# A half unit's start: TensorE's own count in place of a pass through ScalarE, and sums of h by either engine

## Chip, cores and metric

The kernel runs on one core of a Trainium2 chip. The metric is device time in microseconds (us) for one execution. A core has five engines with a queue each, which work side by side and wait for each other through semaphores: TensorE (PE in the profile, with its weight loads as PEld), VectorE (DVE), ScalarE (ACT), GpSimd (POOL) and SyncE (SP, which issues the DMAs).

## What is computed

One transformer layer with attention and an MLP in parallel, on 2048 tokens of width 512; 32 heads of 16, hidden width 1792:

```python
xn = _layernorm(x, axis=-1)
return x + _A_ref(xn, A_wqkv, A_wo) + _B_ref(xn, B_w1, B_b1, B_w2, B_b2)
# _A_ref: scores = q @ k.T * Dh**-0.5; p = softmax(scores); o = p @ v; o @ wo
# _B_ref: h = gelu(xn @ w1 + b1); h @ w2 + b2
```

## The kernel before

Attention is cut into 512 *units*: a group of four heads, a block of 512 queries, a block of 128 keys. For each unit the scores are formed twice. S (`s_half`, four a unit, one per head) has queries on the partitions; DVE takes the row maximum from PSUM (L226). Twenty units later (LEAD) T (`e_half`) forms the transposed scores with the maximum folded in, ACT takes the exponential into a tile pe (L273), and V (`v_half`) multiplies it with the values and adds up over 16 units in one PSUM bank. V is in fp32 and runs as two passes in the trace.

Beside that runs *dense* work, D: groups of products that add up in a bank of their own. In order of time they are 24 groups of the q and k projections, the MLP in four blocks of tokens (14 groups for h, then four for the output y), and the output projection. `Group.pace` says how many D products a half unit takes: four, or three (FAST, MEAN, SLOW). All products use 64 rows of the PE array and 32 columns at a time, so that each shows as four tiles, and two row halves work side by side.

`unit` (L551) writes the order by hand. A unit has two halves; I call each a *block*. A block issues S, T, S, T, then V on one row half of the array and D on the other. In the next block the halves change over. So V and D of a block add into the same banks as those of the block before, from other rows, and must not start before those are finished. For this, an empty instruction is put on DVE or ACT at the end of each block (L579), whichever has the smaller count of work given (`backlog`, from which HALF = 1300 ns is taken per block). It waits for the newest product on PE (L580), and the next block's first product of V or D waits for it (`fence`, L166 to L169). It stands in the engine's queue behind that engine's earlier work.

S and T rotate over three PSUM banks each; D has one, V one. When a D group ends, its bank goes to T's list (`Group.end`), with ACT or DVE still to read it. For h this is `hidden` (L952): DVE scales hp and adds the bias into hh, then ACT and GpSimd do the gelu in later slots.

Of the kernel before, what the change touches and what calls it, by code (L numbers as in the profile page):

```python
# [8 lines left out]
F32 = mybir.dt.float32  # L9
# [8 lines left out]
P = 128  # L18
# [29 lines left out]
def layer_kernel(ctx: ExitStack, tc: tile.TileContext, x, wqkv, wo, w1, b1, w2, b2, out):  # L48
# [43 lines left out]
    nc.gpsimd.memset(vv[:, :, 0:H * VW].rearrange("p t (h e) -> p t h e", e=VW)[:, :, :, DH], 1.0)  # L92
    nc.gpsimd.memset(vv[:, :, H * VW:], 0.0)
    wo_s = const.tile([P, 2, NC, D], F16, name="wo_s")
    wo_l = const.tile([64, 2, D], F16, name="wo_l")
    sexp = const.tile([P, 4], F32, name="sexp")

    mnegs = [const.tile([P, 32], F32, name=f"mneg{i}") for i in range(2)]
# [55 lines left out]

    PAIRS = ((0, 0), (0, 1), (1, 0))

    AFTER = mybir.DependencyInfo(mybir.DependencyClass.Sync, mybir.DependencyReason.DATA)
    fence, newest = [None], [None]

    backlog = {"act": 0, "dve": 0}  # L160

    def given(engine, ns):
        backlog[engine] += ns

    def product(*args, **kw):
        newest[0] = nc.tensor.matmul(*args, **kw)  # L166
        if fence[0] is not None:
            tc.add_manual_dep(newest[0].ins, fence[0].ins.name, AFTER, reason="other rows")
            fence[0] = None  # L169

    def tiled(dst, lhs, rhs, start, stop):

        for j in range(0, P, 32):
            product(dst[j:j + 32], lhs[:, j:j + 32], rhs, start=start, stop=stop)


    mt_of, ptiles, pv_of = {}, {}, {}
# [36 lines left out]
    def s_half(u, n):  # L214

        t, i = divmod(u, 16)
        g, qb = divmod(t, NQB)
        qt, kb = divmod(i, 4) if t else (i % 4, i // 4)
        if t not in mt_of:
            mt_of[t] = work.tile([P, 4, 4, 4], F32, name="mt", bufs=2)  # L220
        ks, qs = kst[g % 2], qst[g % 2]
        p, a = divmod(n, 2)
        r = slice(64 * a, 64 * a + 62)
        s = banks("S")
        tiled(s, qs[p][qb][r, qt * P:(qt + 1) * P], ks[p][kb][r, :], True, True)
        nc.vector.reduce_max(mt_of[t][:, n, qt, kb:kb + 1], s, axis=AX.X)  # L226
        given("dve", 600)

# [33 lines left out]
    def e_half(u, n):  # L262

        p, a = divmod(n, 2)
        t, kt = divmod(u, 16)
        g, qb = divmod(t, NQB)
        st = banks("T")
        r = slice(64 * a, 64 * a + 64)
        k0 = (kt % 4) * P
        tiled(st, kst[g % 2][p][kt // 4][r, k0:k0 + P], qst[g % 2][p][qb][r, :], True, True)  # L270
        pe = work.tile([P, QB], F32, name="pe", bufs=10)
        ptiles[u, n] = pe
        nc.scalar.activation(pe, st, AF.Exp, scale=sexp[:, g // 2:g // 2 + 1])  # L273
        given("act", 580)

    def v_half(u, a):

        t, kt = divmod(u, 16)
        g, qb = divmod(t, NQB)
        if kt == 0 and a == 0:  # L280
            pv_of[t] = hold("V", "S")
        pv = pv_of[t][0]
        r = slice(64 * a, 64 * a + 64)
        for h in (2, 3, 0, 1):
            c = (4 * g + h) * VW
            product(pv[32 * h:32 * h + 32, :], vv[r, kt, c:c + 32], ptiles[u, h][r],
                    start=(kt == 0 and a == 0), stop=(kt == 15 and a == 1))

    def v_end(u):
# [90 lines left out]
    class Group:  # L380
# [15 lines left out]
        def product(self, side):  # L396

            if self.bank is None:
                self.bank, self.key = self.alloc()
            lhs, rhs = self.prods[side % 2][self.at[side % 2]]()  # L400
            start = self.first and self.at == [0, 0]
            if side == 2:
                self.at = [min(self.at[0] + 1, n) for n in self.n]
                nc.tensor.matmul(self.bank, lhs, rhs, start=start, stop=self.last and self.over())  # L404
                return
            r = slice(64 * side, 64 * side + 64)
            self.at[side] += 1
            tiled(self.bank, lhs[r], rhs[r], start, self.last and self.over())

        def over(self):  # L410
            return self.at == self.n
# [40 lines left out]
    def project(m, w, sb, wh, bank, early=False):  # L452

        prods = [lambda c=c, i=i, j=j: (wh[:, w, i, c, :], xt[:, j, c, sb * QB:(sb + 1) * QB])
                 for c in range(NC) for i, j in PAIRS]

        dst = qk_d[w, m * P:(m + 1) * P, :, sb * QB:(sb + 1) * QB]

        def finish(pj):
            def put():  # L460
                nc.sync.dma_start(dst[:, w:w + 2, :], stg)
                nc.sync.dma_start(dst[:, 2 - 2 * w, :], stg[:, 0])

            stg = work.tile([P, 2, QB], F16, name="stg", bufs=2)
            given("act", 600)
            if early or (w == 1 and not m):
                nc.scalar.activation(stg[:, 0], pj, AF.Copy)
                nc.vector.tensor_tensor(stg[:, 1], pj, stg[:, 0], op=ALU.subtract)
            else:
                pf = ph.tile([P, QB], F32, name="pf", bufs=2)  # L470
                nc.scalar.activation(pf, pj, AF.Copy)
                if not m:
                    nc.scalar.activation(stg[:, 0], pj, AF.Copy)
                    nc.gpsimd.tensor_tensor(stg[:, 1], pf, stg[:, 0], op=ALU.subtract)
                else:
                    hi = lambda: nc.gpsimd.tensor_scalar(stg[:, 0], pf, 1.0, 0.0, op0=ALU.mult, op1=ALU.add)
                    lo = lambda: nc.gpsimd.tensor_tensor(stg[:, 1], pf, stg[:, 0], op=ALU.subtract)
                    later(1, lambda: pooled((620, hi), (1160, lo), (0, lambda: later(1, put, True))), True)
                    return

            put()

        return Group(prods, bank, finish)
# [62 lines left out]
                    cur[0].product(side)  # L546
        ended()

    passed_by = [None]

    def unit(gen):  # L551


        u = pos[0]
        e = u - LEAD
        if u == LEAD and cur[0] is not None:
            burst(gen, cur[0].left())
        pos[0] += 1
        for a in range(2):
            for b in range(2 * a, 2 * a + 2):  # L560
                if u < NU:
                    s_half(u, b)
                if 0 <= e < NU:
                    e_half(e, b ^ 1)
            if e >= 0:
                fence[0] = passed_by[0]

                w, r = (e - 2, 1) if a == 0 else (e - 1, 0)
                live = 0 <= w < NU
                new = r == 0 and w % 16 == 0  # L570
                if live and not new:
                    v_half(w, r)
                dense(gen, 1 - r)
                if live and new:
                    v_half(w, r)

                for k in backlog:
                    backlog[k] = max(0, backlog[k] - HALF)
                passed_by[0] = (nc.vector if backlog["dve"] < backlog["act"] else nc.scalar).nop()  # L579
                tc.add_manual_dep(passed_by[0].ins, newest[0].ins.name, AFTER, reason="block")  # L580
                if live and r == 1:
                    v_end(w)
                ended()
        if u < NU:
            s_end(u)
        if u < LEAD:
            burst(gen, LFILL[u - 16])
        tick()
# [9 lines left out]
    with ExitStack() as st1:  # L598
# [240 lines left out]
        def prepare():  # L839
# [20 lines left out]
            for n in range(16):  # L860
                v = fetch(16 + n)
                while not ended[0]:
                    yield
                ended[0] = False

                def then(wh=None, n=n):
                    ended[0] = True
                    if n < 7:
                        for a in range(2):
                            for l in range(2):  # L870
                                nc.sync.dma_start(w1_d[2 * n + a][:, l], wh[:, l, :, a * P:(a + 1) * P])
                    elif n < 14:
                        nc.sync.dma_start(w2_d[:, :, 2 * n - 14:2 * n - 12, :], wh)
                    elif n == 15:
                        nc.sync.dma_start(wo_l, wo_s[64:128, :, NC - 1, :])

                if n >= 14:
                    i = 2 * (n - 14)
                    split_steps(wo_s[:, 0, i:i + 2, :], wo_s[:, 1, i:i + 2, :], v, inv[:, 9:10], then)
                    continue  # L880
                wh = ph.tile([P, 2, 4, W] if n < 7 else [P, 2, 2, D], F16, name="wsp", bufs=2)
                k = n if n < 7 else 8
                split_steps(wh[:, 0], wh[:, 1], v, inv[:, k:k + 1], lambda wh=wh, then=then: then(wh))
# [12 lines left out]
    def mlp():  # L896
# [43 lines left out]
        for b in range(NQB):  # L940
            xb = xbs[b]
            g = m2.tile([P, 2, NF, QB], F16, name="g", bufs=1)
            for f in range(NF):
# [8 lines left out]
                def hidden(hp, g=g, b=b, f=f):  # L952
                    hh = m2.tile([P, QB], F32, name="hh", bufs=3)
                    scale, bias = fac1[0][:, f // 2:f // 2 + 1], b1_s[:, f:f + 1]
                    nc.vector.tensor_scalar(hh, hp, scale, bias, op0=ALU.mult, op1=ALU.add)  # L955
                    given("dve", 700)
                    later(1, lambda: gelu(hh, g, b, f), True)

                yield Group([lambda c=c, i=i, j=j, wc=wc, xb=xb: (wc[:, i, c, :], xb[:, j, c, :])
# [74 lines left out]
        flush()  # L1034
    with ExitStack() as st3:
        p3 = pool(st3, "ph3")

        blocks = {}

# [64 lines left out]
```

## Time and profile before

| | |
|---|---|
| median of 3 runs | 1587.66 us (1586.63 to 1590.76) |
| the profiled execution | 1592.59 us, its span 1590.8 us |
| row maximum, L226 on DVE | 2048 of them, 1293.2 us busy |
| exponential, L273 on ACT | 2048 of them, 1270.1 us busy |
| V on PE, L166 | 8192 rows (4 tiles, two passes), 1083.3 us busy |
| hh, L955 on DVE | 56 of them, 45.4 us busy |

A group's row gives busy time, mean duration in ns and, behind the bar, the idle time of its engine just before it and what ended that. A timeline row gives start, duration, engine, line, operation, out<-in, shape and count, and in brackets idle time and its releaser. "who waited" rows give total and count. Nearly all matmuls have line L166, since a helper issues them; the tile's name tells them apart (pS, pT, pV, pD).

### The profile page before, as it was taken

Reading aid. Unit: us, or ns where it says so; the run is one execution under the profiler, and the core shown is the slowest. Engines: PE = TensorE matmul, PEld = TensorE weight load, DVE = VectorE, ACT = ScalarE, POOL = GpSimd, SP = SyncE. Lnnn points to the kernel's source line nnn. Section 1 sums busy time; section 2 is a strip of 40 time slices with the busy share of each in tenths; the row PEclk is TensorE's granted clock in tenths of the full one; section 3 lists DMA queues with packets and bytes.
Section 4 is the critical chain, followed back from the end, with each engine's and each line's share of the span. In section 5 each row is a group of like instructions: output and inputs, shape, how many; then the busy total and the mean of one; then the engine's idle time right before and its main releaser. Section 6 shows DMA issues by size and latency. Waiting matters only on the chain.

```text
span 1590.8 us, 86996 instructions
## 1 busy us (share of the span) xinstructions
PE 1535.3 (97%) x38915; PEld 807.7 (51%) x38915; DVE 1424.0 (90%) x2388; ACT 1378.9 (87%) x2254; POOL 668.7 (42%) x742
## 2 busy tenths in 40 slices
PE   8997998999999999999999999999999999999998
PEld 4433554545555555555455555555555555554443
DVE  7896987989999999999899999999999999999901
ACT  4315997989999999999899999999999999999893
POOL 3113586727773111677411157681116775211000
PEclk9999999999999999999999999999999999999999
DMA  6466375361112111121111111221112110103222
GB/s 204 136 210 210 108 190 184 124 197 53 44 54 64 35 34 31 55 60 46 46 38 48 33 53 41 61 67 33 33 46 59 41 34 15 39 23 97 91 95 82
DMA packets 120256, 123.78 MB, mean 78 GB/s; under 512 B 38988, under 2 KB 90572, under 8 KB 119880
## 3 DMA queue, kind: packets, MB, share of 16 engines
q1 hardware_dynamic: 119880, 118.21, 24.6%
q8 instruction: 304, 4.98, 1.3%
q14 instruction: 72, 0.59, 0.1%
HBM read 80.61 MB, written 37.34 MB: 74 GB/s over the span
## 4 chain that ended last, share of the span: by engine, by line
PE 80%; DVE 10%; DMA 4%; POOL 2%; issue 2%; SPq 1%; ACT 1%; DVEq 0%; ACTq 0%; POOLq 0%
PE pV L166 25%; PE pD L166 18%; PE pT L166 17%; PE pS L166 16%; DVE mt L226 6%; DVE hh L955 2%; PE pD L404 1%; DMA wch<-in_B_w_dram 1%; PE pT L404 1%; DVE amx L614 1%; DMA dn<-den_d 1%; PE pT L497 1%; ACT pe L273 0%; DMA m_d<-mhl 0%; DMA xb<-xn_d 0%
## 5 line engine op out<-in xcount | busy, mean ns | idle before, releaser
L226 DVE TENSOR_REDUCE mt<-pS 128x1 f32<-128x512 f32 x2048 | 1293.2, 683 | 59.4 <-PE pS L166 34.3
L273 ACT ACTIVATE pe<-pT,sexp 128x512 f32<-128x512 f32 x2048 | 1270.1, 686 | 77.5 <-PE pT L166 27.9
L166 PE MATMUL pV<-pe,vv 64*32 64x512 f32 x8192 | 1083.3, 599 | 1.9 <-ACTq L579 0.8
L166 PE MATMUL pT<-qst,kst 64*32 64x512 f16 x8192 | 708.1, 379 | 11.3 <-DMA qst<-m_d 8.2
L166 PE MATMUL pS<-kst,qst 62*32 62x512 f16 x8192 | 640.9, 379 | 28.0 <-DVE mt L226 24.1
L166 PEld LDWEIGHTS <-qst 62*32 62x32 f16 x8192 | 271.5, 92 | 253.2 <-issue 123.0
L166 PEld LDWEIGHTS <-kst 64*32 64x32 f16 x8192 | 290.9, 91 | 209.4 <-issue 80.2
L166 PE MATMUL pD<-w_s,g 64*32 64x512 f16 x5376 | 365.4, 379 | 0.0
L166 PE MATMUL pD<-xb,wc 64*32 64x512 f16 x5376 | 360.9, 378 | 0.2 <-issue 0.2
L166 PEld LDWEIGHTS pV<-pe,vv 64*32 64x32 f32 x8192 | 177.0, 105 | 122.4 <-ACTq L579 25.4
L166 PEld LDWEIGHTS <-wc 64*32 64x32 f16 x5376 | 117.4, 92 | 46.0 <-issue 2.3
L166 PEld LDWEIGHTS <-g 64*32 64x32 f16 x5376 | 106.9, 92 | 44.2 <-issue 0.7
L166 PE MATMUL pD<-xt,wqk_h 64*32 64x512 f16 x1920 | 127.4, 381 | 0.7 <-issue 0.7
L973 POOL TENSOR_TENSOR xa<-xa,yt 128x512 f32<-128x512 f32 x16 | 20.4, 1276 | 242.9 <-ACT yt L971 242.9
L935 POOL TENSOR_TENSOR t<-hh 128x512 f32<-128x512 f32 x56 | 58.2, 1039 | 119.3 <-DVE hh L955 117.8
L324 POOL TENSOR_TENSOR osb<-osb,rb 128x512 f32<-128x512 f32 x31 | 39.8, 1284 | 157.0 <-DMA rb<-den_d 115.1
L250 POOL TENSOR_SCALAR mhl<-msb 64x64 f16<-64x64 f32 x32 | 7.6, 236 | 178.4 <-DVE msb L247 178.4
L937 POOL TENSOR_TENSOR t<-t,hh 128x512 f32<-128x512 f32 x56 | 71.7, 1280 | 4.7
L930 POOL TENSOR_TENSOR t<-t,hh 128x512 f32<-128x512 f32 x56 | 71.5, 1277 | 4.7
L932 POOL TENSOR_TENSOR g<-t,g 128x512 f16<-128x512 f32 x56 | 65.1, 1163 | 4.4
L166 PE MATMUL pD<-wo_s,oc 64*32 64x512 f16 x768 | 50.8, 378 | 0.8 <-issue 0.8
L166 PEld LDWEIGHTS <-wqk_h 64*32 64x32 f16 x1920 | 43.0, 92 | 16.7 <-issue 1.9
(138 smaller groups left out, 868.0 us busy)
## 6 DMA issues: line engine op xcount, KB each, us to landing
wch<-in_B_w_dram SPq DMA_DIRECT2D x28, 512.0 KB
wc<-w_d SPq DMA_DIRECT2D x56, 256.0 KB
qk_d<-stg SPq DMA_DIRECT2D x32, 256.0 KB
rb<-den_d SPq DMA_DIRECT2D x124, 64.0 KB
kst<-qk_d SPq DMA_DIRECT2D x128, 48.0 KB
qst<-qk_d SPq DMA_DIRECT2D x128, 48.0 KB
xs<-in_A_x_dram SPq DMA_DIRECT2D x16, 256.0 KB
qk_d<-stg SPq DMA_DIRECT2D x32, 128.0 KB
```

Of the source, the lines that this page charges most:

```text
L166: newest[0] = nc.tensor.matmul(*args, **kw)
L226: nc.vector.reduce_max(mt_of[t][:, n, qt, kb:kb + 1], s, axis=AX.X)
L273: nc.scalar.activation(pe, st, AF.Exp, scale=sexp[:, g // 2:g // 2 + 1])
L324: pooled((1280, lambda: nc.gpsimd.tensor_tensor(osb, osb, rb, op=ALU.mult)), (620, lambda: nc.gpsimd.tensor_scalar(ot[:, 0], osb, 1.0, 0.0 ...
L404: nc.tensor.matmul(self.bank, lhs, rhs, start=start, stop=self.last and self.over())
L497: nc.tensor.matmul(pj, xt[:, i, c, t * P:(t + 1) * P], wh[j][:, c, :], start=(n == 0), stop=(n == 11))
L930: (1280, lambda: nc.gpsimd.tensor_tensor(t1, t1, hh, op=ALU.mult)),
L932: (1160, lambda: nc.gpsimd.tensor_tensor(g[:, 1, f, :], t1, g[:, 0, f, :], op=ALU.subtract)),
L935: pooled((1040, lambda: nc.gpsimd.tensor_tensor(t1, hh, hh, op=ALU.mult)), (620, lambda: nc.gpsimd.tensor_scalar(t1, t1, 1.0, 1.0 / GELU_A ...
L937: (1280, lambda: nc.gpsimd.tensor_tensor(t1, t1, hh, op=ALU.mult)),
L955: nc.vector.tensor_scalar(hh, hp, scale, bias, op0=ALU.mult, op1=ALU.add)
L973: add = lambda: nc.gpsimd.tensor_tensor(xa, xa, yt, op=ALU.add)
```

## The change

The empty instruction, the fence and its two dependencies go. In their place PE counts: at the end of a block (`leave`) the newest product of each user (V, D) and each column quarter adds 1 to a semaphore `turns`, if that user's sum goes on; before the next V or D (`enter`) PE waits until `turns` has reached the count. What depended on those products now depends on that wait. `hidden` gives its operation to ACT or DVE, whichever has less in `backlog`. pe has 12 buffers instead of 10; for the space, wo_l moves into the last stage's pool, with its DMA, and stg into the first stage's.

```diff
-    def product(*args, **kw):
-        newest[0] = nc.tensor.matmul(*args, **kw)
-        if fence[0] is not None:
-            tc.add_manual_dep(newest[0].ins, fence[0].ins.name, AFTER, reason="other rows")
-            fence[0] = None
+    def product(key, *args, **kw):
+        p = nc.tensor.matmul(*args, **kw)
+        if key[0] is not None:
+            newest[key] = p
+    def leave(user, goes_on):
+        for key in [k for k in newest if k[0] == user]:
+            p = newest.pop(key)
+            if goes_on:
+                p.then_inc(turns, 1)
+                tc.no_tile_sem_insts.add(p.ins.name)
+                counted[0] += 1
+                waits[0].append(p)
+    def enter():
+        if waits[0]:
+            group = f"turn{counted[0]}"
+            for p in waits[0]:
+                tc.add_to_no_dep_group(group, p.ins)
+            w = nc.tensor.wait_ge(turns, counted[0])
+            tc.declare_fence(w.ins, group=group)
+            waits[0] = []
...
-        pe = work.tile([P, QB], F32, name="pe", bufs=10)
+        pe = work.tile([P, QB], F32, name="pe", bufs=12)
...
             if e >= 0:
-                fence[0] = passed_by[0]
+                enter()
...
+                for user, goes_on in (("V", live and not (r == 1 and w % 16 == 15)),
+                                      ("D", cur[0] is not None and not cur[0].over())):
+                    leave(user, goes_on)
                 for k in backlog:
                     backlog[k] = max(0, backlog[k] - HALF)
-                passed_by[0] = (nc.vector if backlog["dve"] < backlog["act"] else nc.scalar).nop()
-                tc.add_manual_dep(passed_by[0].ins, newest[0].ins.name, AFTER, reason="block")
...
-                    nc.vector.tensor_scalar(hh, hp, scale, bias, op0=ALU.mult, op1=ALU.add)
-                    given("dve", 700)
+                    if backlog["act"] < backlog["dve"]:
+                        nc.scalar.activation(hh, hp, AF.Identity, scale=scale, bias=bias)
+                        given("act", 800)
+                    else:
+                        nc.vector.tensor_scalar(hh, hp, scale, bias, op0=ALU.mult, op1=ALU.add)
+                        given("dve", 800)
...
         p3 = pool(st3, "ph3")
+        wo_l = p3.tile([64, 2, D], F16, name="wo_l")
+        nc.sync.dma_start(wo_l, wo_s[64:128, :, NC - 1, :])
```

What stands on PE at the start of V and D of a block in the MLP's second half, before:

```order
L166 MATMUL pT<-qst_0_3_108,kst_0_2_91 32x512
L166 MATMUL pV<-pe,vv 32x512 [waits Activation_sequencer_49]
L166 MATMUL pV<-pe,vv 32x512 x3
L166 LDWEIGHTS g
L166 MATMUL pD<-w_s,g 32x512
```

and at the same place with the change (the names in brackets are semaphores):

```order
L169 MATMUL pT<-qst_0_3_108,kst_0_2_91 32x512
L169 MATMUL pV<-pe,vv 32x512 [waits turns]
L169 MATMUL pV<-pe,vv 32x512 x3
L169 LDWEIGHTS g
L169 MATMUL pD<-w_s,g 32x512
```

The matmuls keep their places in all 1027 blocks; what V waits for is another semaphore, that of PE's own count, and the wait is an instruction of its own just ahead of V (it has no row).

On DVE, around the fourth to sixth sums of h, before:

```order
L247 TENSOR_SCALAR msb<-pS 64x64 [waits PE_49]
L226 TENSOR_REDUCE mt<-pS 128x1 [waits PE_49] x8
L955 TENSOR_SCALAR hh<-pD,fac_2454,b_s 128x512 [waits PE_49,Pool_49]
L226 TENSOR_REDUCE mt<-pS 128x1 [waits PE_49] x16
L955 TENSOR_SCALAR hh<-pD,fac_2454,b_s 128x512 [waits PE_49,Pool_49]
L226 TENSOR_REDUCE mt<-pS 128x1 [waits PE_49] x12
```

With the change, a stretch of the same stage on DVE, and the fifth hh on ACT (L975; L943 is the gelu's tanh):

```order
L269 TENSOR_SCALAR msb<-pS 64x64 [waits PE_49,Pool_49]
L248 TENSOR_REDUCE mt<-pS 128x1 [waits PE_49] x36
L336 RECIPROCAL dn<-dn 64x32 [waits DMAHW5_49,DMAHW1_49]
L248 TENSOR_REDUCE mt<-pS 128x1 [waits PE_49] x24
L259 TENSOR_REDUCE mneg_119<-mt 128x16 [waits DVE_49]
```

```order
L295 ACTIVATE pe<-pT,sexp 128x512 [waits PE_sequencer_49,PE_49,Activation_49]
L295 ACTIVATE pe<-pT,sexp 128x512 [waits PE_49] x3
L975 ACTIVATE hh<-pD,b_s,fac_2452 128x512 [waits PE_49,Pool_49]
L943 ACTIVATE t_9561<-t_9561 128x512 [waits Pool_49]
L295 ACTIVATE pe<-pT,sexp 128x512 [waits PE_sequencer_49,PE_49,Activation_49]
```

DVE's row maxima follow each other without a sum of h between them; 54 of the 56 sums stand on ACT, two (the 54th and 55th) on DVE. Some stand right ahead of a tanh. The first exp of a unit now also waits for PE's wait instruction (PE_sequencer), which tells that the old content of its pe buffer has been read.

More of the change, by code (lines that the diff above doesn't have):

```diff
@@ L94, in layer_kernel @@
     wo_s = const.tile([P, 2, NC, D], F16, name="wo_s")
-    wo_l = const.tile([64, 2, D], F16, name="wo_l")
     sexp = const.tile([P, 4], F32, name="sexp")
@@ L155, in layer_kernel @@
     PAIRS = ((0, 0), (0, 1), (1, 0))
-    AFTER = mybir.DependencyInfo(mybir.DependencyClass.Sync, mybir.DependencyReason.DATA)
-    fence, newest = [None], [None]
     backlog = {"act": 0, "dve": 0}
@@ L163, in given, with tiled @@
         backlog[engine] += ns
-    def product(*args, **kw):
-        newest[0] = nc.tensor.matmul(*args, **kw)
-        if fence[0] is not None:
-            tc.add_manual_dep(newest[0].ins, fence[0].ins.name, AFTER, reason="other rows")
-            fence[0] = None
-    def tiled(dst, lhs, rhs, start, stop):
+    turns = tc.alloc_semaphore("turns")
+    counted, waits, newest = [0], [[]], {}
+    def product(key, *args, **kw):
[18 more added lines that the diff above has]
+            waits[0] = []
+    def tiled(user, dst, lhs, rhs, start, stop):
         for j in range(0, P, 32):
-            product(dst[j:j + 32], lhs[:, j:j + 32], rhs, start=start, stop=stop)
+            product((user, j), dst[j:j + 32], lhs[:, j:j + 32], rhs, start=start, stop=stop)
     mt_of, ptiles, pv_of = {}, {}, {}
@@ L224, in s_half @@
         s = banks("S")
-        tiled(s, qs[p][qb][r, qt * P:(qt + 1) * P], ks[p][kb][r, :], True, True)
+        tiled(None, s, qs[p][qb][r, qt * P:(qt + 1) * P], ks[p][kb][r, :], True, True)
         nc.vector.reduce_max(mt_of[t][:, n, qt, kb:kb + 1], s, axis=AX.X)
@@ L269, in e_half @@
         k0 = (kt % 4) * P
-        tiled(st, kst[g % 2][p][kt // 4][r, k0:k0 + P], qst[g % 2][p][qb][r, :], True, True)
-        pe = work.tile([P, QB], F32, name="pe", bufs=10)
+        tiled(None, st, kst[g % 2][p][kt // 4][r, k0:k0 + P], qst[g % 2][p][qb][r, :], True, True)
+        pe = work.tile([P, QB], F32, name="pe", bufs=12)
         ptiles[u, n] = pe
@@ L285, in v_half @@
             c = (4 * g + h) * VW
-            product(pv[32 * h:32 * h + 32, :], vv[r, kt, c:c + 32], ptiles[u, h][r],
+            product(("V", h), pv[32 * h:32 * h + 32, :], vv[r, kt, c:c + 32], ptiles[u, h][r],
                     start=(kt == 0 and a == 0), stop=(kt == 15 and a == 1))
@@ L407, in product @@
             self.at[side] += 1
-            tiled(self.bank, lhs[r], rhs[r], start, self.last and self.over())
+            tiled("D", self.bank, lhs[r], rhs[r], start, self.last and self.over())
         def over(self):
@@ L462, in put @@
                 nc.sync.dma_start(dst[:, 2 - 2 * w, :], stg[:, 0])
-            stg = work.tile([P, 2, QB], F16, name="stg", bufs=2)
+            stg = ph.tile([P, 2, QB], F16, name="stg", bufs=2)
             given("act", 600)
@@ L547, in land @@
         ended()
-    passed_by = [None]
     def unit(gen):
@@ L873, in then @@
                         nc.sync.dma_start(w2_d[:, :, 2 * n - 14:2 * n - 12, :], wh)
-                    elif n == 15:
-                        nc.sync.dma_start(wo_l, wo_s[64:128, :, NC - 1, :])
                 if n >= 14:
```

## The prediction

> **What bounds the kernel now.** I read the page's totals and chain first, then the half-unit pitch, then single blocks.
>
> ```profile
> PE 1535.3 (97%) x38915; PEld 807.7 (51%) x38915; DVE 1424.0 (90%) x2388; ACT 1378.9 (87%) x2254; POOL 668.7 (42%) x742
> ...
> PE 80%; DVE 10%; DMA 4%; POOL 2%; issue 2%; SPq 1%; ACT 1%; DVEq 0%; ACTq 0%; POOLq 0%
> ```
>
> TensorE (PE) looks full, 97% busy, but PE time in a page is from a matmul's start to its modelled end, and eight tiles overlap. So I look for what starts a half unit, here called a block. The empty instruction of L579 stands once in each:
>
> ```profile
> L579 ACTq EVENT_SEMAPHORE  x1027: 17/17/17, 137.3 to 1568.0; - x172
> ```
>
> All 1027 went to ScalarE (ACT). (1568.0 - 137.3) / 1026 = 1.394 us is the mean block, and these 1431 us are nine tenths of the span. Two stretches, one with three D products a block (12 tiles) and one with four (16 tiles), the latter past the last S:
>
> ```profile
> L579 ACTq EVENT_SEMAPHORE  x21: 17/17/17, 520.0 to 545.9; - x21
> ...
> L579 ACTq EVENT_SEMAPHORE  x17: 17/17/17, 1530.9 to 1552.2; - x17
> ...
>   PEld pV L166: 7.9, 17
> ```
>
> 25.9 / 20 = 1.295 us and 21.3 / 16 = 1.331 us, very regular. In the second, V's weight load waited 7.9 us in 17 blocks for L579, 0.46 us each. There PE has room, and still no block is shorter:
>
> ```profile
> 1532.30 0.63 PE L166 MATMUL pV<-pe,vv 64*32 64x512 f32 x4
> 1532.33 0.61 PE L166 MATMUL pD<-wo_s,oc 64*32 64x512 f16 x8
> 1532.75 0.61 PE L166 MATMUL pV<-pe,vv 64*32 64x512 f32 x4
> 1532.77 0.60 PE L166 MATMUL pD<-wo_s,oc 64*32 64x512 f16 x8
> 1533.18 0.41 PE L166 MATMUL pT<-qst,kst 64*32 64x512 f16 x8
> 1533.63 0.63 PE L166 MATMUL pV<-pe,vv 64*32 64x512 f32 x4
> ```
>
> V's second pass ends at 1532.75 + 0.61 = 1533.36 and the last D at 1533.37; V of the next block starts at 1533.63. Nothing else was due, so the block is a loop: V runs, V and D are reported complete, ACT passes that on, V may start. With 12 tiles:
>
> ```profile
> 800.49 0.61 PE L166 MATMUL pV<-pe,vv 64*32 64x512 f32 x4
> 800.50 0.39 PE L166 MATMUL pD<-w_s,g 64*32 64x512 f16 x4
> 800.72 0.39 PE L166 MATMUL pT<-qst,kst 64*32 64x512 f16 x4
> 800.91 0.41 PE L166 MATMUL pS<-kst,qst 62*32 62x512 f16 x8
> 801.13 0.40 PE L166 MATMUL pT<-qst,kst 64*32 64x512 f16 x4
> 801.33 0.63 PE L166 MATMUL pV<-pe,vv 64*32 64x512 f32 x4
> ```
>
> D ended at 800.89, V at 801.10, the next V started at 801.33: 0.23 us after V's end, against 0.27 with 16 tiles. D's tiles had long ended and still count: they are reported behind V, one after the other. Four tiles more make a block 1.331 - 1.295 = 0.036 us longer, 9 ns each. **An update of a semaphore costs more than a tile:**
>
> ```profile
> 158.81 0.40 PE L166 MATMUL pS<-kst,qst 62*32 62x512 f16 x4
> 158.83 0.60 PE L166 MATMUL pT<-qst,kst 64*32 64x512 f16 x8
> ...
> 159.26 0.69 DVE L226 TENSOR_REDUCE mt<-pS 128x1 f32<-128x512 f32 x1 [0.17 <-PE pT L166]
> 159.32 0.69 ACT L273 ACTIVATE pe<-pT,sexp 128x512 f32<-128x512 f32 x1 [0.43 <-PE pT L166]
> ```
>
> The eight tiles of S and the first T run side by side, and both readers stood idle. VectorE (DVE) gets its S at 159.26, ACT its T 0.06 us later. Between the two reports lie four tiles and one update: 60 - 4 x 9 = about 25 ns for the update.
>
> The blocks over the floor: 1.394 less the mean floor of 1.313 is 0.081, x 1027 = 83 us of stalls. Many are in the four stages that compute h:
>
> ```profile
> L579 ACTq EVENT_SEMAPHORE  x90: 17/17/17, 635.0 to 760.3; - x90
> ...
> 660.00:760.00 100.00, 97.97 (x2696) 53.21 (x2682) 96.80 (x159) 93.18 (x155) 74.77 (x81) 1.00 0.18 50
> ```
>
> 125.3 / 89 = 1.408 us a block, with DVE 97% and ACT 93% busy: there DVE has almost no room.
>
> **The change, part by part.** The sum is made against the profiled execution, 1592.59 us (span 1590.8 us and 1.8 us around it); the median of the runs, 1587.66 us, is 4.9 us lower, and I carry the difference over to it.
>
> 1. The wait. It no longer passes through ACT: away goes the empty instruction (17 ns, row above) and the way to it and back. In its place stands a wait of PE's own, an instruction by itself. The trace has four such waits on PE:
>
> ```profile
> L166 PEldq EVENT_SEMAPHORE  x4: 51/51/51, 37.6 to 1565.3; - x4
> ```
>
> Saved are between 0.017 us (the instruction alone) and 0.07 us (two crossings of about its own length with it, an estimate); spent are 0 (if it overlaps V's wake-up) to 0.051 us. The net lies between -0.07 and +0.034 us a block; I take 0, as V's wake-up, now part of the 0.23 us, is paid once either way. Behind the waiting PE instruction stand V, D and the S and T of the next block, as before.
>
> 2. The updates. Before, V and D of a block made one update, on the last D tile. Now the four V tiles and the last D tile of each column quarter make one each: eight, hence **seven more**. They are reported in order behind V's end, so they lie in the loop: 7 x 25 = 175 ns. Bounds from the rows: 0 each, and 60 ns each if the whole distance of the two reports were the update: 0 to 0.42 us a block. I take 25, since the 9 ns for a tile are measured apart.
>
> [...]
>
> 3. How many blocks pay. The wait asks only for users that go on: D is left out in the block that ends a group (24 + 56 + 16 groups and a few of the output projection, about 100) and in some 35 without D; V in 32. About 1027 - 135 - 32 = 860 wait for both: 860 x 0.175 = +150 us. The others lose or gain some hundredths each, put at nothing.
>
> 4. h.
>
> ```profile
> L273 ACT ACTIVATE pe<-pT,sexp 128x512 f32<-128x512 f32 x2048 | 1270.1, 686 | 77.5 <-PE pT L166 27.9 <-PE pS L166 20.9 <-ACT pe L273 0.3
> ...
> L955 DVE TENSOR_SCALAR hh<-pD,fac,b_s 128x512 f32<-128x512 f32 x56 | 45.4, 810 | 1.2
> ...
> L971 ACT ACTIVATE yt<-pD,gs 128x512 f32<-128x512 f32 x16 | 11.0, 690 | 0.2 <-PE pT L166 0.2
> ```
>
> The program's order settles who gets them: the planner's count of DVE is ahead from the sixteen early units, where nothing is deducted, so 54 of the 56 go to ACT. DVE loses 54 x 0.81 = 44 us, ACT gains 54 x 0.69 = 37 us (L971, same shape and kind of operands, is the nearest row). Beside a loop of 1.47 us and more this is hidden: an exp costs ACT 1270.1 / 2048 = 0.62 us, two a block 1.24.
>
> 5. What is given back. With longer blocks DVE and ACT catch up, and a block that already stood 0.2 us late pays little more. Of the 83 us, all could vanish (+67 in sum) or none (+150). In h stages ACT would be at 93 + 7 (37 us over 510 us of stages) = 100% of the old length, some 95% of the new: tight, so a few stalls stay, and those for DMAs too. I take 70 us back: +150 - 70 = **+80 us**.
>
> 6. The rest at nothing: two more pe buffers cover that an exp now waits for PE's wait one block later (three units of four exps, where V is two units behind); stg only changes its pool. The copy into wo_l moves on SP's queue from 302.6 us to behind the last MLP store, with the loads of oc after it:
>
> ```profile
> L875 SPq DMA_DIRECT2D wo_l<-wo_s x1: 642/642/642, 302.6 to 302.6; - x1
> ```
>
> Its issue takes 0.64 us, and its reader is the last projection, over 100 us later; without this cover it would cost its landing, a few us.
>
> Sum: 1592.59 + 80 = 1673 us for a profiled execution, 1587.66 + 80 = **1668 us** for the median.
>
> **Rivals.**
> - *Updates that hide, faster.* If an update costs nothing extra (for it: no row shows two in succession without tiles between) and PE's wait replaces the hop free of charge, the block falls to what V and the two S/T rounds take in the rows of 800.49: 2 x 0.43 + 2 x 0.21 = 1.28 us, from 1.313: 1027 x 0.033 = 34 us less. Against it: the 9 ns slope and the 0.06 us. **1554 us.** It needs updates under some 12 ns: 860 x 7 x 12 ns = 72 us, what the stalls give back.
> - *ACT becomes the bound, slower by little.* Updates hide, but 37 us more on ACT, 93% busy in the h stages, leave it no idle time; the stages lengthen by 1 to 6% of 510 us, some 12 us. **1600 us.** Against it: exps can run closer, 0.62 us against a duration of 0.686.
> - *Each update costs the whole 0.06 us.* 860 x 0.42 = 361, less 80 of stalls, +281: **1869 us.** Against it: the 9 ns a tile are seen apart.
>
> **How the numbers follow.** The forecast has 0.74; its own range is 1604 (updates of 20 ns in 860 blocks, +120, all stalls given back and hop savings of 0.025 us) to 1738 (+150, none given back). Hiding has 0.10, ACT as bound 0.08, the dear update 0.08. The range must leave out at most 0.2: the two far ends, 0.18, stay out, the 1600 comes in: 1595 to 1740. A measurement of this kernel tells 0.3% (5 us) from no change. Faster: 0.10 + 0.01; same: 0.03 of the second rival and 0.02 of the forecast's low end; slower: the rest, 0.84.
>
> **What would show it.** Waits of PE at the new wait's line, about 1027; blocks of about 1.47 us (12 tiles) and 1.51 (16), where V's end and the next V lie 0.40 to 0.45 us apart, not 0.23 to 0.27; the two readers still 0.06 us apart; DVE's busy time down by 44 us, ACT's up by 37, both shares falling as the span grows. Wrong: blocks of 1.29 us or less with eight updates in them (then updates are free), of 1.7 (then dear), or h stages alone getting longer, with ACT at 99%.

## The result and the profile after

| | before | changed |
|---|---|---|
| median | 1589.21 us (1586.63 to 1590.77) | 1776.28 us (1774.18 to 1779.68) |
| ratio | 1 | 1.118 (95% interval 1.1155 to 1.1207) |

The change costs 187 us; +80 was forecast. The page's totals of the changed kernel, busy time and share of the span by engine:

```profile
span 1772.4 us, 87015 instructions
...
PE 1701.6 (96%) x38915; PEld 873.3 (49%) x38915; DVE 1410.9 (80%) x2334; ACT 1424.5 (80%) x2308; POOL 669.5 (38%) x742
```

PE is still "96% busy", while DVE and ACT both fell to 80%: they are less of a limit than before, and wait for PE. What stands ahead of each block is now PE's own wait, L189. Its row in the whole span, and in two regular stretches, one of 12 tiles a block and one of 16 (kind, count, duration in ns as least, median and most, first and last start in us):

```profile
L189 PEldq EVENT_SEMAPHORE  x1027: 51/51/51, 139.5 to 1750.1; - x172
...
L189 PEldq EVENT_SEMAPHORE  x12: 51/51/51, 864.7 to 881.2; - x12
...
L189 PEldq EVENT_SEMAPHORE  x6: 51/51/51, 1655.1 to 1662.7; - x6
```

The mean block is (1750.1 - 139.5) / 1026 = 1.570 us, against 1.394. The regular ones take 16.5 / 11 = 1.50 us (1.295 before) and 7.6 / 5 = 1.52 us (1.331). By the single records of the trace the floors, that is the length which regular blocks keep to, are 1.495 and 1.528 us, both 0.20 us up. PE in two such blocks:

```profile
880.22 0.63 PE L169 MATMUL pV<-pe,vv 64*32 64x512 f32 x3
880.26 0.38 PE L169 MATMUL pD<-w_s,g 64*32 64x512 f16 x1
880.27 0.59 PE L169 MATMUL pV<-pe,vv 64*32 64x512 f32 x1
...
880.91 0.38 PE L169 MATMUL pS<-kst,qst 62*32 62x512 f16 x2
881.29 0.63 PE L169 MATMUL pV<-pe,vv 64*32 64x512 f32 x4
...
881.72 0.63 PE L169 MATMUL pV<-pe,vv 64*32 64x512 f32 x3
```

V's second pass ends at 880.22 + 0.63 = 880.85, and the next V starts at 881.29: 0.44 us where 0.23 stood before. The last S and T in between start by 880.91, so 0.38 us pass in which PE starts nothing. The forecast for V's end to the next V was 0.40 to 0.45 us. Who waited (us in total, times, longest):

```profile
PEld pV L169 <- issue: 259.5, 827, 3.4
...
DVE mt L248 <- PE pS L169: 135.0, 395, 3.5
```

"issue" is the own wait seen from V's weight load: the view can name nothing that released the load, since the wait that held it up is an instruction of its own ahead of it. In 856 blocks both V and D go on (the semaphore is raised by 8 in 856 blocks and by 4 in the other 171). There a floor higher by 0.199 us makes 170 us. By the forecast 70 us of stalls should have gone off that; instead the total is 17 us more.

### The profile page after: what moved, and what is told of

Read it like the earlier page. It is cut to its first block, busy times and chain, and to the rows that moved or that the text cites. A ratio compares the mean times of both kernels' runs of the same rounds, so it can differ in the third digit from the quotient of the medians.

```text
span 1772.4 us, 87015 instructions
## 1 busy us (share of the span) xinstructions
PE 1701.6 (96%) x38915; PEld 873.3 (49%) x38915; DVE 1410.9 (80%) x2334; ACT 1424.5 (80%) x2308; POOL 669.5 (38%) x742
## 4 chain that ended last, share of the span: by engine, by line
PE 74%; issue 2%; ACT 2%; DVE 0%; POOL 0%; SPq 0%; DMA 0%; DVEq 0%; ACTq 0%; POOLq 0%
PE pV L169 29%; PE pT L169 15%; PE pD L169 15%; PE pS L169 14%; ACT pe L295 1%; ACT t L943 1%; PE pD L426 1%; PE pS L426 0%; DVE mt L248 0%; DVE ac L1017 0%; SPq L353 0%; ACT hh L975 0%; DMA qst<-m_d 0%; POOL osb L346 0%; PE pS L266 0%
## 5 line engine op out<-in xcount | busy, mean ns | idle before, releaser
L248 DVE TENSOR_REDUCE mt<-pS 128x1 f32<-128x512 f32 x2048 | 1315.9, 685 | 239.3 <-PE pS L169 135.0
L295 ACT ACTIVATE pe<-pT,sexp 128x512 f32<-128x512 f32 x2048 | 1284.8, 688 | 212.0 <-ACT pe L295 98.8
L169 PE MATMUL pV<-pe,vv 64*32 64x512 f32 x8192 | 1114.1, 597 | 17.1 <-issue 8.9
L169 PE MATMUL pT<-qst,kst 64*32 64x512 f16 x8192 | 744.3, 378 | 16.9 <-ACT pe L295 10.7
L169 PE MATMUL pS<-kst,qst 62*32 62x512 f16 x8192 | 674.0, 379 | 21.2 <-DVE mt L248 15.9
L169 PEld LDWEIGHTS <-kst 64*32 64x32 f16 x8192 | 314.5, 91 | 212.8 <-issue 73.1
L169 PEld LDWEIGHTS <-qst 62*32 62x32 f16 x8192 | 280.6, 92 | 203.1 <-issue 71.0
L169 PE MATMUL pD<-w_s,g 64*32 64x512 f16 x5376 | 372.1, 379 | 0.3 <-issue 0.2
L169 PE MATMUL pD<-xb,wc 64*32 64x512 f16 x5376 | 367.8, 379 | 3.2 <-DMA wc<-w_d 2.1
L169 PEld LDWEIGHTS pV<-pe,vv 64*32 64x32 f32 x8192 | 203.7, 104 | 269.7 <-issue 259.5
L996 POOL TENSOR_TENSOR xa<-xa,yt 128x512 f32<-128x512 f32 x16 | 20.4, 1275 | 275.1 <-ACT yt L994 275.1
```

What stands on the lines that cost most here:

```text
L169: p = nc.tensor.matmul(*args, **kw)
L996: add = lambda: nc.gpsimd.tensor_tensor(xa, xa, yt, op=ALU.add)
```

## The experiments

Each kernel ran beside the kernel before on the same chip. "Floor" is the time from V to V in regular blocks with 12 tiles, taken from the trace. With the old fence these take 1.290 or 1.302 us, and 1.296 is the mean of the two. The two kernels with V and D apart have no sharp floor, and the median stands there.

| run | median us | ratio (95%) | floor us |
|---|---|---|---|
| changed, one update a block | 1661.99 | 1.0449 (1.0421 to 1.0476) | 1.332 |
| changed, twelve updates | 1847.34 | 1.1612 (1.1582 to 1.1642) | 1.598 |
| changed, h on DVE | 1785.33 | 1.1218 (1.1197 to 1.1239) | 1.495 |
| before, h on ACT | 1598.05 | 1.0047 (1.0031 to 1.0063) | 1.296 |
| before, V's and D's fence apart | 1574.42 | 0.9883 (0.9859 to 0.9907) | 1.251 |
| changed, one update, wait on V's product | 1574.41 | 0.9873 (0.9853 to 0.9893) | 1.264 |
| changed, but with before's fence | 1599.77 | 1.0042 (1.0028 to 1.0056) | 1.296 |
| before, and an own wait already met | 1610.32 | 1.0104 (1.0084 to 1.0123) | 1.296 |
| two counts, waits on products, h on DVE | 1554.40 | 0.9748 (0.9726 to 0.9771) | 1.24 |
| changed, seven updates, wait on V's product | 1658.59 | 1.0399 (1.0376 to 1.0422) | 1.405 |
| changed, one update, wait on V's product, h on DVE | 1564.92 | 0.9819 (0.9799 to 0.9839) | 1.264 |

Where times of different rows are subtracted, it is their ratios, times 1590 us.

**One update, and twelve.** Theory 1: each update costs 26 ns in the loop (the semaphore's records of the changed kernel fit 25.7) and the rest of the change next to nothing. Theory 2: PE's own wait is dear. Theory 3: the sums of h on ACT are. Here only the last product of a block raises the count:

```diff
+            newest.pop(key, None)
             newest[key] = p
...
-                    leave(user, goes_on)
+                on = {"V": live and not (r == 1 and w % 16 == 15), "D": cur[0] is not None and not cur[0].over()}
+                last_of = [k for k in newest if on[k[0]]][-1:]
+                kept = {k: newest[k] for k in last_of}
+                newest.clear()
+                newest.update(kept)
+                for k in last_of:
+                    leave(k[0], True)
```

> The changed kernel, but PE's count is raised by one product of a block alone, the last one of V or D whose sum goes on, instead of by eight. Theory 1 (each update takes 26 ns of the loop, seven more take 0.16 us; PE's own wait costs 0.04 us more than the pass through ACT): blocks of 1.33 us with 12 tiles and 1.37 with 16 instead of 1.495 and 1.528, 860 blocks shorter by 0.16, about 1635 us. Theory 2 (PE's own wait, which holds up its whole queue, is what costs): blocks stay near 1.49, 1775 us. Theory 3 (sums of h on ACT cost most of the surplus over the forecast, the updates the rest): about 1690 us.

For twelve, the product before the newest of each column quarter of D counts too:

```diff
+            if key[0] == "D" and key in newest:
+                newest["D", key[1], "next"] = newest[key]
```

> The changed kernel, but the last two D products of each column quarter raise PE's count, so 12 updates a block in place of 8 where D goes on. Theory 1: four more updates, 0.104 us more in about 890 blocks, about 1868 us, blocks of 1.60 and 1.63 us. Theory 2: as the changed kernel, 1776 us. Theory 3: between, if updates cost less than 26 ns each.

Floors 1.332, 1.495 and 1.598 us with 1, 8 and 12 updates: 0.163 / 7 = 23 ns and 0.103 / 4 = 26 ns an update. The size of an update is settled. (Twelve came to 1847 us, 21 below the 1868 of theory 1, though the floor is as forecast: some stalls were given back.) But with one update, as many as before, the kernel still lost 71 us; the higher floor gives 856 x 0.036 = 31 of them. Theory 1 was not the whole.

**The sums of h.** In the changed kernel all on DVE; in the kernel before all on ACT.

```diff
-                    if backlog["act"] < backlog["dve"]:
+                    if False:
...
-                    nc.vector.tensor_scalar(hh, hp, scale, bias, op0=ALU.mult, op1=ALU.add)
-                    given("dve", 700)
+                    nc.scalar.activation(hh, hp, AF.Identity, scale=scale, bias=bias)
+                    given("act", 800)
```

> The changed kernel with all sums of h on DVE, as before the change. Theory 1: within 15 us of the changed kernel, 1760 to 1790 us, since DVE is 80% busy there and takes 44 us back. Theory 2: the same. Theory 3 (h on ACT costs): shorter by 40 to 80 us, 1700 to 1735 us.

> The kernel before with all sums of h on ACT, nothing else changed. Theory 1: within 15 us of the kernel before, 1575 to 1605 us. Theory 2: the same. Theory 3: 40 to 80 us slower, 1630 to 1670 us.

On ACT the sums cost the kernel before 7 us (there the planner also moved the empty instruction to DVE in 125 of 1027 blocks, which this includes), and taking them off ACT made the changed kernel no faster (1.1218 against 1.1181): theory 3 falls as the cause of the loss.

**The wait on a product, and the rest of the change by itself.** In the run with one update blocks stood still for which no semaphore could answer. Its weight loads (start, duration, and in brackets the idle time of the weight loads before it):

```profile
559.43 0.10 PEld L169 LDWEIGHTS <-kst 64*32 64x32 f16 x2
559.68 0.17 PEld L169 LDWEIGHTS pV<-pe,vv 64*32 64x32 f32 x4 [0.16 <-issue]
560.52 0.11 PEld L169 LDWEIGHTS pV<-pe,vv 64*32 64x32 f32 x2 [0.67 <-issue]
560.53 0.10 PEld L169 LDWEIGHTS <-g 64*32 64x32 f16 x4
```

The wait was over at 559.66 and V's first loads were issued at 559.68, but the next weight loads came 0.84 us later, D's with them. Nothing in between waits for a semaphore. I counted such gaps: over 0.3 us between starts of matmuls or weight loads, with none of the semaphores that the next instructions wait for released in the 0.13 us ahead. What a gap lasts beyond 0.216 us, about the time from one round of four tiles to the next, is added up. The last column tells where in PE's stream of instructions the gaps lie, modulo 256 (77830 weight loads and matmuls of the kernel before over the 304 packets shown below):

```
kernel                               gaps   us over 0.216 each   in places 160 to 223 of 256
before                                78        16.9                 22
before, own wait already met         120        34.4                 48
changed, one update                  161        48.2                124
changed                              181        52.7                131
changed, one update, wait on V        89        20.4                 20
changed, seven updates, wait on V     59        17.1                 16
```

Two of eight places hold three quarters of the gaps where PE waits by an instruction of its own, two fifths where that wait is always met, and a quarter where there is none. The row of an instruction queue on the page says what comes in such portions (packets, MB), first before, then with one update:

```profile
q8 instruction: 304, 4.98, 1.3%
...
q8 instruction: 308, 5.05, 1.3%
```

It has 304 packets in every kernel without an own wait in each block and 308 in every kernel with one, so it brings PE's instructions: 2 x 38915 weight loads and matmuls and 1027 waits are 78857, 256 for each of 308 packets.

The trace also has the time of each packet. Most gaps of the own wait lie at five places, 189 to 193, which PE passes about 300 times after its first block:

```
kernel                               passed with a gap   its end after the last packet's end   passed without, after it
before                                  7 of 298                     1.39                             2.98
before, own wait already met           30 of 302                     1.40                             2.16
changed, one update                    94 of 302                     1.43                             1.85
changed                               100 of 302                     1.37                             1.63
changed, one update, wait on V         10 of 298                     1.40                             2.82
changed, seven updates, wait on V       6 of 298                     1.39                             3.11
```

The times are medians, in us. With a gap or without, PE passed this place less than 1.2 us behind a packet's end in at most 10 of the 302 passes of a kernel, and most gaps end 1.2 to 1.6 us behind it. Without the own wait PE comes there 1.4 to 1.7 us later than the gaps end, which is the lead of the supply; an open own wait leaves 0.3 to 0.4 us of it. So the gaps belong to the fetch of instructions. Which packet carries which instructions, and what passes between its end and the first start, the trace doesn't tell.

Why an open own wait takes away from this lead, no row shows. Theory 2 took a new form, an assumption of mine that stands in the next expectation, and the next runs put what follows from it to the test: the wait carried by V's first product, the old fence in the changed kernel, and an own wait that never waits in the kernel before.

```diff
         p = nc.tensor.matmul(*args, **kw)
+        if due[0] is not None and key[0] is not None:
+            p._wait_ge(turns, counted[0])
+            tc.declare_fence(p.ins, group=due[0])
+            due[0] = None
...
-            w = nc.tensor.wait_ge(turns, counted[0])
-            tc.declare_fence(w.ins, group=group)
+            due[0] = group
```

> As the run with one update a block, but the wait for the count is carried by the first V product of the block instead of by an instruction of PE's own. Theory 2 in its new form (a wait that is an instruction of its own stops PE from taking in what stands behind it, so that its supply with instructions isn't hidden): the gaps on PE that nothing releases fall back from 161 to about 78 and the floor from 1.33 to 1.20 to 1.28 us, below before's 1.296, as no other engine passes the count on: 1520 to 1580 us. If the own wait is no dearer than a wait on a product (theory 1 alone), and the stalls come from something else in the change, it stays at 1640 to 1665.

The same one update, 92 us less. The floor falls from 1.332 to 1.264, worth 856 x 0.068 = 58 us, and the gaps from 48.2 to 20.4 us, worth 28: 86 of the 92. PE at the same place of the block as above, and the last V of the same regular stretch:

```profile
520.27 0.63 PE L169 MATMUL pV<-pe,vv 64*32 64x512 f32 x4
...
520.73 0.61 PE L169 MATMUL pV<-pe,vv 64*32 64x512 f32 x4
520.76 0.39 PE L169 MATMUL pD<-w_s,g 64*32 64x512 f16 x4
...
521.37 0.40 PE L169 MATMUL pT<-qst,kst 64*32 64x512 f16 x4
521.53 0.63 PE L169 MATMUL pV<-pe,vv 64*32 64x512 f32 x4
...
543.01 0.64 PE L169 MATMUL pV<-pe,vv 64*32 64x512 f32 x4
```

18 blocks from 520.27 to 543.01 are 1.263 us each, and the next V starts 521.53 - 521.34 = 0.19 us after V's end, with T issued right up to it.

The old fence in the changed kernel:

```diff
-                enter()
+                fence[0] = passed_by[0]
...
-                    leave(user, goes_on)
...
+                passed_by[0] = (nc.vector if backlog["dve"] < backlog["act"] else nc.scalar).nop()
+                tc.add_manual_dep(passed_by[0].ins, newest[0].ins.name, AFTER, reason="block")
```

> The changed kernel with before's fence: one nop on VectorE or ScalarE behind the last product, no count, no wait of PE's own; twelve buffers of P, wo_l and stg placed as changed, sums of h as changed (nearly all on ScalarE). If the whole loss lies in the updates and in PE's own wait, as theories 1 and 2 have it, it is what before with h on ScalarE was: 1590 to 1605 us. If the buffers or the late load of wo_l carry a part of it, 1610 to 1660.

With 1.0042 the buffers, wo_l, stg and h together cost 7 us, as h alone did in the kernel before. All else lies in the count and its wait. Now the kernel before with an own wait from the second block on, for a count that is reached at the end of the first:

```diff
                 fence[0] = passed_by[0]
+                if marked:
+                    nc.tensor.wait_ge(spare, 1)
...
+                if not marked:
+                    marked.append(nc.scalar.nop().then_inc(spare, 1))
```

> Before, with one more instruction on PE ahead of each block's V products: a wait for a count that was reached at the first block, so that it never has to wait. If an own wait is dear only while it stays open, nothing behind it being taken in, the time stays at 1585 to 1600 us. If the instruction by itself stops the supply, or costs its 51 ns a block in any case, 1620 to 1660 us (1027 x 51 ns = 52 us).

It came out between the two expectations: 17 us, a third of 1026 x 51 ns. The floor didn't move, so the 51 ns cost nothing where V then waits for the old fence anyway; the gaps grew by 34.4 - 16.9 = 17.5 us, which is all of it. An own wait disturbs the supply even when met, and 1.6 to 1.9 times as much when it stays open (48.2 and 52.7 us of gaps, less the 20.0 of the changed kernel with the old fence).

**The updates without the own wait.** All updates of the changed kernel but V's for head 2, with the wait on V's first product.

> The changed kernel with seven of its eight updates (that of V's product for head 2 is left away), and the wait on the first V product instead of an instruction of PE's own. Beside the run with one update and the wait on the product (1574 us, floor 1.264) this adds six updates: by theory 1 the floor rises by 6 x 26 ns less what the products in order pay anyway, near 0.14 us, to 1.40, and 856 x 0.14 = 120 us, less 25 us of stalls given back: 1660 to 1695 us. If the updates are dear only together with PE's own wait, it stays below 1620.

Its floor is up by 1.405 - 1.264 = 0.141 us, 23.5 ns for each of six more updates, and it has no more gaps than before. So the two costs are apart and add up in the floor. Its rows, with the next V 1.41 us behind the first:

```profile
534.59 0.63 PE L169 MATMUL pV<-pe,vv 64*32 64x512 f32 x4
534.62 0.61 PE L169 MATMUL pD<-w_s,g 64*32 64x512 f16 x8
535.04 0.60 PE L169 MATMUL pV<-pe,vv 64*32 64x512 f32 x3
...
536.00 0.63 PE L169 MATMUL pV<-pe,vv 64*32 64x512 f32 x4
```

In time the six cost 84 us, where 856 x 0.141 = 121: 37 us of stalls were given back, 12 more than expected, so the 1658.6 us lie just below the expected range.

**What beats both.** In the kernel before, V's next start waits for D's report, which comes after V's: by the semaphore's records of the changed kernel, D's first update stands 0.101 us (median) behind V's last. Two nops on ACT, one behind V and one behind D:

```diff
...
+                for user, goes_on in (("V", live and not (r == 1 and w % 16 == 15)),
+                                      ("D", cur[0] is not None and not cur[0].over())):
+                    if goes_on and user in newest:
+                        passed_by[user] = nc.scalar.nop()
+                        tc.add_manual_dep(passed_by[user].ins, newest[user].ins.name, AFTER, reason="block")
```

> Before, with two nops on ScalarE in the place of one: one behind the last V product, on which the next V waits, and one behind the last D product, on which the next D waits; a user that starts a new sum waits for none. If the 0.10 us a block that lie between the last D product and the next V are what before pays (theory 1, the report's way there and back), they go for the 856 blocks that pay: floors near 1.20 us, where before's blocks without a dense product stand, and 1500 to 1540 us in all. If VectorE and ScalarE (73 and 70% busy before) are late as soon as the floor falls, the time ends between, 1550 to 1585. If a second nop a block holds ScalarE up more than it saves, 1590 to 1630.

The median block fell to 1.251, not to 1.20, and the time to 1574 us, the case in between. (The busy shares before, 73 and 70% in the expectation, are 90 and 87% on the page of the kernel before: the readers had less room than the expectation says.) The page's chain by engine shows DVE with 15%, where it had 10%:

```profile
PE 76%; DVE 15%; DMA 4%; POOL 2%; issue 2%; ACT 1%; SPq 1%; DVEq 0%; ACTq 0%; POOLq 0%
```

Next, the wait on the product with h on DVE:

> As the run with one update a block and the wait on the first V product, with the sums of h on VectorE as in before. Sums on ScalarE cost 7.5 us in before and gained 9 us in the changed kernel, so 1560 to 1585 us: the choice of engine is worth 10 us at most either way.

It came to 1565 us, within what was expected: h on DVE is worth 9 us here. Then both ideas together, a count for V and one for D, raised by the last product of each and waited for by the first of the next block:

```diff
+        if user in due:
+            p._wait_ge(turns[user], counted[user])
+            tc.declare_fence(p.ins, group=due.pop(user))
...
+        p = newest.pop(user, None)
+        if goes_on and p is not None:
+            p.then_inc(turns[user], 1)
```

> Two counts in the place of one: the last V product of a block raises V's, the last D product D's, and the first V and the first D product of the next block wait for them; sums of h on VectorE again. If what was gained in the two runs before adds up (users apart: floors 1.25 for 1.30; the wait on a product, no engine between: 1.264 for 1.30), and a second update costs 26 ns a block (22 us), the floor is near 1.22 to 1.25 and the time 1540 to 1570 us. If PE's own work sets the pitch once the two users are apart (1.19 to 1.22 us a block without any wait), or VectorE and ScalarE are late more often, nothing is left to win and the second update is lost: 1570 to 1600 us.

At 1554.4 us, in the middle of the first case, it is 2.5% faster than the kernel before. Two of its blocks:

```profile
335.24 0.63 PE L169 MATMUL pV<-pe,vv 64*32 64x512 f32 x4
335.40 0.61 PE L169 MATMUL pD<-xb,wc 64*32 64x512 f16 x8
...
336.49 0.66 PE L169 MATMUL pV<-pe,vv 64*32 64x512 f32 x4
336.56 0.61 PE L169 MATMUL pD<-xb,wc 64*32 64x512 f16 x8
...
337.67 0.63 PE L169 MATMUL pV<-pe,vv 64*32 64x512 f32 x4
```

1.25 and 1.18 us, and D now starts 0.07 to 0.16 us behind V, for it has a wait of its own. So what the change was made of, PE counting for itself, does pay: with one update for each user, on a product that is there anyway.

## Why the prediction was right and wrong

The direction and the loop were right, and the size was 108 us short (1776 against 1668). By its steps:

| step | forecast us | measured us | from |
|---|---|---|---|
| 1, the wait in place of the hop | 0 | +65 | ratio 1.0449 less 1.0042 |
| 2 and 3, seven updates in 860 blocks | +150 | +140 | 0.163 us x 856 blocks |
| 5, stalls given back | -70 | -24 | (1.1181 - 1.0449) x 1590 less 140 |
| 4 and 6, h and the rest | 0 | +7 | ratio 1.0042 |
| sum | +80 | +188 | |

**Step 1 failed, and most.** It set the saved hop against the 51 ns of the own wait and took 0, with 0.034 us a block as the worst. The floor rose by 0.036, just past that bound, worth 31 us. The semaphore's records show where (medians): from the last update to the start of PE's wait 28 ns, from there to V 107, together 135; before, from the last update to the nop 22 and from the nop to V 74, together 96. (The other bound, 0.07 us saved, doesn't follow from its words either: three lengths of 17 ns are 0.051.) But the step asked only what the instruction takes, not what gaps come with it; the 28 us of them (48.2 against 20.0 in the changed kernel with the old fence) were not in the sum at all. These two make 59 of the 65 us; the other 6 stay open. The step did say that V, D and the next S and T stand behind the waiting instruction "as before". They didn't: before, the wait sat on V's product itself. The two order excerpts ahead of the prediction read alike but for the semaphore's name, and that the wait was an instruction of its own stood only in a sentence below them.

**Steps 2 and 3 held.** An update took 23 to 26 ns in the loop (25 forecast), in 856 blocks (860). The spacing of the semaphore's records in the changed kernel (medians of 34 ns between D's updates, 42 between V's, 101 from V's last to D's first) fits 8.3 ns a tile and 25.7 ns an update; the 9 from the two stretches and the 25 from the two readers 0.06 us apart were near. Of the 171 other blocks, put at nothing, the 51 without D rose from 1.196 to 1.292 us, 5 us in all.

**Step 4 held in size.** The row of h on ACT and the two left on DVE:

```profile
L975 ACT ACTIVATE hh<-pD,b_s,fac x54: 777/778/806, 368.0 to 1466.6; 128x512 f32<-128x512 f32 x54
L978 DVE TENSOR_SCALAR hh<-pD,fac,b_s x2: 804/806/809, 1445.5 to 1457.3; 128x512 f32<-128x512 f32 x2
```

54 of 56 went to ACT, at 0.778 us instead of 0.69. ACT's busy time rose by 45.6 us (37 forecast), and DVE's fell by 13.1 instead of 44, for the larger part because its row maxima grew by 23 (first before, then changed):

```profile
L226 DVE TENSOR_REDUCE mt<-pS 128x1 f32<-128x512 f32 x2048 | 1293.2, 683 | 59.4 <-PE pS L166 34.3
...
L248 DVE TENSOR_REDUCE mt<-pS 128x1 f32<-128x512 f32 x2048 | 1315.9, 685 | 239.3 <-PE pS L169 135.0
```

Its last field is the better sign: DVE now stood idle 239.3 us just before row maxima, where it had been 59.4, and there was room for h on either engine.

**Step 5 was mis-sized.** It let 70 of 83 us of stalls vanish. By the same count, the blocks' time over their floors, there were 88 us before and 93 after. Of the 88, gaps without any semaphore were 17; of the 93 they were 53. So the other stalls did shrink, from 71 to 40, and the own wait added new ones that no longer block covers, since they are PE's own.

**The rivals.** Hidden updates fell with the floor. ACT as the bound fell with its 80%. The dear update, 60 ns, came nearest in time (1869 us, 93 off), but by luck: its floor would be 1.7 us, and 1.495 was measured.

## What to carry to other kernels

Put a semaphore wait on the instruction that needs it. A wait that is an instruction of its own on a busy TensorE cost here 0.068 us a block in the chain (58 us in all) and another 28 us in gaps of supply that no view names but as "issue". Let each independent user raise a count once, on its last product, and let it be waited for apart. When a stall is to be given back by longer blocks, ask first whose it is: here the other stalls shrank from 71 to 40 us, and the gaps of PE, which sets the pitch, grew from 17 to 53.

## What the runs showed of the hardware that I had not expected

- Instruction supply shows on PE: gaps of some 0.4 us where its stream passes one place in every 256 instructions, in 94 to 100 of 302 passes with an open own wait, 30 with a met one, 6 to 10 of 298 without. Most end 1.2 to 1.6 us behind the end of the last instruction packet, whatever the kernel.
- V's first weight load shows 0.03 us ahead of V where the wait is PE's own (881.26 and 881.29 in the changed kernel), and beside it where V carries the wait (521.53 both). The wait on the product thus seems to cover the load too, which would be a part of the 0.068 us between the two floors; no run tests it alone.
- The path through another engine was not dear: V's start by way of an empty instruction on ACT came 96 ns after the last update, by an own wait of PE 135 ns. Where V itself waits for the count, its first weight load comes 42 to 43 ns after it.
